# DeltaNet with soft-MoE slots on one core: two heads on tiles of 64x64 for three of TensorE's products, their weights made on GpSimd

## The chip, the cores and the metric

The kernel runs on one core of a Trainium2 chip. The metric is device time in microseconds (us) from the first to the last instruction, taken as the median of several executions. The engines are named as the profile names them: PE is TensorE's matmul, PEld its weight load, DVE is VectorE, ACT is ScalarE, POOL is GpSimd, SP is SyncE, which issues most transfers.

## The reference

Two blocks are computed one after the other, all in float32: attention with a delta rule, then a soft mixture of experts by slots.

```python
# attention: B=4, H=8, S=768, D=48
k_n = k / (np.linalg.norm(k, axis=-1, keepdims=True) + 1e-06)
for t in range(S):
    y[:, :, t] = q_t @ state
    v_old = k_t @ state
    state = state + beta_t * outer(k_t, v_t - v_old)
# bridge: x = y as (B*S, H*D) = (3072, 384)
# moe: 8 experts, 4 slots each, F = 1024
logits = x @ phi
d = softmax of logits over the 3072 rows          # for each of 32 slots
slot_input = d.T @ x                              # 32 x 384
slot_out[e] = relu(slot_input[e] @ w1[e]) @ w2[e]
c = softmax of logits over the 32 slots
out = c @ slot_out
```

(The loop's body is abridged; all heads and batches are computed alike.)

## The kernel before

Time is cut into 24 chunks of 32 steps; 4 chunks are a group, so there are 6 groups. Each 128-row tile holds 4 heads of 32 steps each, and a second index `u` of 8 counts 4 batches and 2 sets of heads. Within a chunk the delta rule is a triangular system. Its inverse (transposed, in `TT`) is made for all 32 systems of a group at once by elimination steps on VectorE, while the group before is in the recurrence.

The recurrence of one chunk, on TensorE, with ScalarE and VectorE reading its results:

```python
def rest():      # v minus what the state already gives for k
    state(0, ks)                                   # 16 matmuls, L413
    nc.vector.tensor_tensor(R, Vt.pop(cc), ks..., op=ALU.subtract)      # L420

def solve():     # L426: one matmul of 128x128 for each u, block-diagonal over 4 heads
    for u in range(U):
        nc.tensor.matmul(pw[:, u], lhsT=Tb[cc % NT][:, u, :], rhs=st["R"][:, u], ...)
    nc.scalar.activation(st["U"], pw, ACT.Copy)    # L429

def read():
    state(1, qs)                                   # L413, for q

def update():    # L439: the state's sum, 16 matmuls on 32 rows; then ACT reads it, L446
    ... lhsT=K[hs[h], b * G:(b + 1) * G, :]  (128 columns) ...

def outputs():   # L455: one matmul of 32x32 for each u and head
    ... lhsT=at[hs[h], b, g, 1, :], rhs=st["U"][hs[h], b * G + g] ...
```

`Tb` is a tile of zeros into whose four diagonal blocks POOL copies the inverse, chunk by chunk:

```python
def weights(cc):                                   # L394
    for h in range(4):
        r = slice(C * h, C * h + C)
        nc.gpsimd.tensor_copy(Tb[cc % NT][r, :, r], TT[n][r, c * U:(c + 1) * U, :])
```

The weights of the outputs, products of k and q, are masked in place on VectorE (`mask`, L246). An elimination step is a product (L321) and a subtraction (L324) on VectorE; the norms of k (L272 to L303), and two scalings of the matrix by `gamma` on POOL (L313), belong to it as well. The steps are spread over three places in each chunk by a table:

```python
share = [(0.0, 0.09, 0.12), (0.09, 0.09, 0.10), (0.09, 0.09, 0.10), (0.10, 0.07, 0.06)]
```

Each engine works through its instructions in order, so R of a chunk waits on VectorE until the steps put ahead of it are done.

One group later the routing follows: logits, the softmax over rows with a running maximum, and the sum of each slot's input. `heads` spreads the weights `pd` over four heads in `dr`, which holds zeros in the other heads' columns; `slots` then sums over rows:

```python
def heads():                                       # L567, 4 ACT instructions
    for h in range(4):
        nc.scalar.activation(dr[:, :, h, :], pd, ACT.Identity, scale=hm[:, h:h + 1])

def slots():                                       # L574, 16 matmuls of 128x128
    for c in range(GC):
        for b in range(B):
            nc.tensor.matmul(pa, lhsT=st["dr"][:, c * B + b]..., rhs=Yn[:, c, b, 0:GD + 1], ...)
```

After the last chunk the experts' weights w1 and w2 (1.5 MB for each expert and layer) are loaded into tiles that lie where attention's tiles lay; the two layers and the outputs follow (L847, L871, L897).

## Time and profile before

| what | before |
|---|---|
| median of 3 runs | 432.43 us (430.94 to 437.08) |
| span of the profiled execution | 435.1 us, mean granted TensorE clock 0.822 |
| first to last solution (L426) | 49.5 to 345.3 us |
| end of the last slots' sum (L574) | about 367 us |
| end of the last load of w2 | 407.7 us |

The profile is a page of one execution, and the trace behind it can be asked for single stretches. A row of the page's groups names line, engine, operation, what is written and read with its shape, and how often; then the busy time in all and the mean duration of one in ns; then how long the engine stood idle just before these instructions and what ended the waits. A row of a timeline gives start and duration in us, engine, line and operation, and in brackets the idle time before it and its releaser; `x16` means that 16 records were merged. A float32 matmul leaves two records, one for each pass through the array: the 16 records of a solution are 8 matmuls. The clock row (PEclk) shows for each of 40 equal slices of the span the clock that TensorE was granted, in tenths of full speed, with 9 for 90% or more.

### The profile page before, as it was taken

The page shows a single profiled execution, that of the slowest core. Times are in us where ns is not written, and L with a number is a line of the kernel's source. Part 1 is how long each engine was busy: PE and PEld are TensorE (multiplying, and loading weights), DVE is VectorE, ACT ScalarE, POOL GpSimd, SP SyncE. Part 2 cuts the span into 40 slices and gives each one's busy share as a digit, 9 for nine tenths or more (in the row PEclk, how much of TensorE's full clock was granted, in tenths as well). Part 3 has the DMA queues.
Part 4 walks back from the last instruction along what each step waited for, and adds up shares of the span by engine and source line. Part 5 has one row for each costly group of instructions (what it writes and reads, how often), then busy time and mean ns, then how long its engine had stood idle before and what let it go on. Part 6 is the DMA issues. An engine that isn't in the chain of part 4 may idle for free.

```text
span 435.1 us, 17057 instructions
## 1 busy us (share of the span) xinstructions
PE 344.3 (79%) x7583; PEld 281.7 (65%) x7583; DVE 226.4 (52%) x574; ACT 153.5 (35%) x308; POOL 103.4 (24%) x192
## 2 busy tenths in 40 slices
PE   4766888988686899779988799586997967876685
PEld 3545778877675897668977689475886856322143
DVE  8493684844858638775586756859502011101033
ACT  3342233455422645236452363331633621201022
POOL 9200702331504045040450404504151000000000
PEclk9999865698957879667995679856899986999595
DMA  6555455144413324342211101111400396799238
GB/s 102 92 89 87 80 86 84 26 67 73 83 23 50 57 43 93 77 106 41 36 22 20 22 10 17 17 20 20 148 3 3 110 431 241 278 427 427 119 127 307
DMA packets 85032, 45.29 MB, mean 104 GB/s; under 512 B 79424, under 2 KB 82656, under 8 KB 83040
## 3 DMA queue, kind: packets, MB, share of 16 engines
q1 hardware_dynamic: 83296, 43.86, 37.7%
q8 instruction: 59, 0.97, 0.9%
q0 software_dynamic: 576, 0.15, 0.3%
q10 hardware_dynamic: 1088, 0.20, 0.2%
q14 instruction: 13, 0.11, 0.1%
HBM read 39.47 MB, written 4.72 MB: 102 GB/s over the span
## 4 chain that ended last, share of the span: by engine, by line
PE 56%; DVE 13%; DMA 10%; ACT 8%; SPq 7%; issue 5%; POOL 1%; DVEq 0%; POOLq 0%; ACTq 0%
PE psR L426 13%; PE psS L439 8%; SPq L82 6%; PE pt L574 6%; DMA w2t<-in_moe_w_dram 5%; PE pt L208 5%; PE psY L455 4%; DVE pr L321 4%; DVE tt L324 3%; PE pso L871 3%; PE psR L413 3%; PE pt L473 3%; PE pt L237 2%; ACT dr L567 2%; DVE R L420 2%
## 5 line engine op out<-in xcount | busy, mean ns | idle before, releaser
L426 PE MATMUL psR<-R,Tb 128*128 128x48 f32 x384 | 61.5, 325 | 31.8 <-DVE R L420 31.8
L426 PEld LDWEIGHTS psR<-R,Tb 128*128 128x128 f32 x384 | 58.5, 241 | 34.8 <-issue 33.1
L321 DVE TENSOR_TENSOR pr<-tt,lb 128x31 f32<-128x31 f32 (+15 forms) x155 | 63.3, 409 | 9.5 <-POOL lb L313 5.2
L324 DVE TENSOR_TENSOR tt<-tt,pr 128x31 f32<-128x31 f32 (+15 forms) x155 | 63.9, 412 | 5.3
L394 POOL COPY Tb<-TT 32x256 f32<-32x256 f32 x96 | 40.8, 425 | 50.3 <-DMA V<-in_v_dram 22.9
L446 ACT ACTIVATE S<-psS 48x768 f32<-48x768 f32 x46 | 37.0, 804 | 30.3 <-PE psS L439 30.0
L429 ACT ACTIVATE U<-psR 128x384 f32<-128x384 f32 x24 | 11.8, 490 | 89.1 <-PE psR L426 78.4
L439 PE MATMUL psS<-U,K 32*128 32x96 f32 x736 | 36.8, 356 | 1.3 <-ACT U L429 0.8
L237 PE MATMUL pt<-KQ 48*32 48x64 f32 (+1 forms) x1792 | 28.0, 237 | 11.8 <-ACT KQ L224 4.7
L439 PEld LDWEIGHTS psS<-U,K 32*128 32x128 f32 x736 | 32.2, 256 | 6.8 <-ACT U L429 3.4
L237 PEld LDWEIGHTS pt<-KQ 48*32 48x32 f32 x1792 | 22.0, 118 | 19.3 <-ACT KQ L224 6.0
L420 DVE TENSOR_TENSOR R<-V,psR 128x384 f32<-128x384 f32 x24 | 13.2, 551 | 37.2 <-PE psR L413 27.4
L241 ACT ACTIVATE GQ<-pt 128x256 f32<-128x256 f32 (+1 forms) x56 | 16.7, 351 | 37.1 <-PE pt L237 37.1
L313 POOL TENSOR_TENSOR tt<-tt,gm 128x512 f32<-128x512 f32 x10 | 11.2, 1123 | 70.8 <-DVE tt L324 70.8
L455 PE MATMUL psY<-U,GQ 32*32 32x48 f32 x1536 | 27.4, 234 | 0.1
L574 PE MATMUL pt<-Y,dr 128*128 128x97 f32 x192 | 25.2, 295 | 2.5 <-ACT dr L567 2.5
L574 PEld LDWEIGHTS pt<-Y,dr 128*128 128x128 f32 x192 | 24.5, 210 | 3.0 <-ACT dr L567 2.8
L413 PE MATMUL psR<-S,KQ 128*32 128x96 f32 x768 | 25.1, 282 | 1.2 <-ACT S L446 1.2
L525 POOL TENSOR_TENSOR Call<-el,sm 128x128 f32<-128x128 f32 x6 | 2.4, 398 | 99.5 <-DVE sm L524 99.5
L455 PEld LDWEIGHTS psY<-U,GQ 32*32 32x32 f32 x1536 | 23.7, 129 | 3.4 <-issue 1.9
L413 PE MATMUL psY<-S,KQ 128*32 128x96 f32 x768 | 23.1, 264 | 0.7 <-issue 0.7
L386 POOL TENSOR_TENSOR V<-V,nT 128x384 f32<-128x384 f32 x24 | 21.0, 876 | 10.0 <-DMA Q<-in_q_dram 7.6
(142 smaller groups left out, 523.2 us busy)
## 6 DMA issues: line engine op xcount, KB each, us to landing
w2t<-in_moe_w_dram SPq DMA_DIRECT2D x8, 1536.0 KB, 17.2
w1t<-in_moe_w_dram SPq DMA_DIRECT2D x7, 1536.0 KB, 9.7
Q<-in_q_dram SPq DMA_DIRECT2D x96, 48.0 KB, 2.7
V<-in_v_dram SPq DMA_DIRECT2D x96, 48.0 KB, 2.4
out_dram<-ob SPq DMA_DIRECT2D x24, 192.0 KB, 2.4
K<-in_k_dram SPq DMA_DIRECT2D x92, 48.0 KB, 2.7
w1t<-in_moe_w_dram SPq DMA_DIRECT2D x3, 512.0 KB, 4.0
bb<-in_beta_dram POOLq DMA_DIRECT2D x16, 6.0 KB, 2.6
```

The costliest lines, as they stand in the source:

```text
L82: eng.dma_start(out=dst[C * h:C * h + C, :, 0:D], in_=src.rearrange("b (g h) s d -> h s (b g) d", h=4)[h, cc * C:(cc + 1) * C])
L237: nc.tensor.matmul(pg[g][rh, b], lhsT=kq[r, b, 0, rh], rhs=kq[r, b, a0:a1, rh], start=True, stop=True, skip_group_check=True)
L321: nc.vector.tensor_tensor(prv, tt[:, j, 0:m].unsqueeze(1).broadcast_to([P, w, m]), lb[:, j, j + 1:C].unsqueeze(2).broadcast_to([P, w, m]), ...
L324: nc.vector.tensor_tensor(tt[:, j + 1:C, 0:m], tt[:, j + 1:C, 0:m], prv, op=ALU.subtract)
L394: nc.gpsimd.tensor_copy(Tb[cc % NT][r, :, r], TT[n][r, c * U:(c + 1) * U, :])
L413: nc.tensor.matmul(dst[hs[h], b].rearrange("p g d -> p (g d)"), lhsT=kq[:, b, a, hs[h]], rhs=old[:, h, b, :], start=(b == 0), stop=False, ...
L420: nc.vector.tensor_tensor(R, Vt.pop(cc), ks.rearrange("p b g d -> p (b g) d"), op=ALU.subtract)
L426: nc.tensor.matmul(pw[:, u], lhsT=Tb[cc % NT][:, u, :], rhs=st["R"][:, u], start=(u == 0), stop=True, skip_group_check=True)
L439: nc.tensor.matmul(psS[:, h, b * GD:(b + 1) * GD], lhsT=K[hs[h], b * G:(b + 1) * G, :].rearrange("p g d -> p (g d)"), rhs=st["U"][hs[h], b ...
L446: nc.scalar.activation(new[r, :, :, g * D:(g + 1) * D], psS[r, :, 0:B * GD].rearrange("p h (b g e) -> p h b g e", b=B, g=G)[:, :, :, g], A ...
L455: nc.tensor.matmul(qs[hs[h], b, g], lhsT=at[hs[h], b, g, 1, :], rhs=st["U"][hs[h], b * G + g], start=False, stop=True, skip_group_check=True)
L574: nc.tensor.matmul(pa, lhsT=st["dr"][:, c * B + b].rearrange("p h s -> p (h s)"), rhs=Yn[:, c, b, 0:GD + 1], start=(c == 0 and b == 0), st ...
```

## The change

It uses the fact that the block-diagonal weights of four heads are half empty even where only two heads are looked at together. Rows 0 to 63 (two heads) and rows 64 to 127 (the other two) become two products of 64x64 that lie on different rows and columns of the array, in place of one of 128x128 (solution, slots) or of four of 32x32 (outputs).

- The solution's and the outputs' weights are made by POOL, in one product each for a chunk: the inverse times `own`, which says which of a row's two columns blocks is its own head's; and the k-q products times `tri`, which holds the causal mask in the own block. The mask on VectorE and the cleared tiles of 128 columns go away.
- The slots' weights need two instead of four instructions on ScalarE. The sum is split into two parts, placed in the last chunk of a group and in the first chunk of the next.
- The update loads 112 instead of 128 columns (the last 16 held padding).
- The next group's norms: the transposition of its products (`spread`) is placed inside the last chunk of a group, the root at that chunk's end, and the rest ahead of R of the next chunk. Before, all of it stood after the chunk and behind that R.
- The table of shares is set anew, and a few preparations in the first four chunks change places.

The diff, cut to its core (cuts are marked with `[...]`):

```diff
+    own = cpool.tile([P, 2], F32, name="own")
+    nc.vector.tensor_reduce(own, hm.rearrange("p (y x) -> p x y", x=2), axis=AX.X, op=ALU.add)
+    tri = cpool.tile([P, 2, C], F32, name="tri")
 [...]
-    Tb = [wk.tile([P, U, P], F32, name=f"Tb{i}", bufs=1) for i in range(NT)]
-    for t in Tb:
-        nc.vector.memset(t, 0.0)
+    Tb = [wk.tile([P, U, 2, C], F32, name=f"Tb{i}", bufs=1) for i in range(NT)]
+    Ab = [wk.tile([P, U, 2, C], F32, name=f"Ab{i}", bufs=1) for i in range(NT)]
 [...]
-        def mask(self):
-            a = GQ[self.n][:, self.c, :, :, 1, :].rearrange("p b g t -> p (b g) t")
-            nc.vector.tensor_tensor(a, a, tri.unsqueeze(1).broadcast_to([P, U, C]), op=ALU.mult)
 [...]
     def weights(cc):
-        for h in range(4):
-            r = slice(C * h, C * h + C)
-            nc.gpsimd.tensor_copy(Tb[cc % NT][r, :, r], TT[n][r, c * U:(c + 1) * U, :])
+        nc.gpsimd.tensor_tensor(
+            Ab[cc % NT], wide(GQ[n][:, c, :, :, 1, :].rearrange("p b g t -> p (b g) t")),
+            tri.unsqueeze(1).broadcast_to([P, U, 2, C]), op=ALU.mult)
+        nc.gpsimd.tensor_tensor(
+            Tb[cc % NT], wide(TT[n][:, c * U:(c + 1) * U, :]),
+            own.unsqueeze(1).unsqueeze(3).broadcast_to([P, U, 2, C]), op=ALU.mult)
 [...]
         def solve():
             for u in range(U):
-                nc.tensor.matmul(pw[:, u], lhsT=Tb[cc % NT][:, u, :], rhs=st["R"][:, u],
-                                 start=(u == 0), stop=True, skip_group_check=True)
+                for y in range(2):
+                    nc.tensor.matmul(pw[half[y], u], lhsT=T[y][:, u], rhs=st["R"][half[y], u],
+                                     start=(u == 0), stop=True, skip_group_check=True)
 [...]
-                        lhsT=K[hs[h], b * G:(b + 1) * G, :].rearrange("p g d -> p (g d)"),
+                        lhsT=K[hs[h], b * G:(b + 1) * G].rearrange("p g d -> p (g d)")[:, 0:DP + D],
 [...]
         def outputs():
-                    for h in range(4):
-                        nc.tensor.matmul(qs[hs[h], b, g], lhsT=at[hs[h], b, g, 1, :],
-                                         rhs=st["U"][hs[h], b * G + g],
+                    for y in range(2):
+                        nc.tensor.matmul(qs[half[y], b, g], lhsT=at[y][:, u],
+                                         rhs=st["U"][half[y], u],
 [...]
         def heads():
-            for h in range(4):
-                nc.scalar.activation(dr[:, :, h, :], ..., ACT.Identity, scale=hm[:, h:h + 1])
+            for x in range(2):
+                nc.scalar.activation(dr[:, :, x, :], ..., ACT.Identity, scale=own[:, x:x + 1])
-        def slots():
+        def slots(cs):
+                    for y in range(2):
+                        r = slice(64 * y, 64 * y + 64)
+                        nc.tensor.matmul(pa[r], lhsT=st["dr"][r, c * B + b]..., rhs=Yn[r, c, b, 0:GD + 1], ...)
 [...]
-                dict(end=[slots]),
-                dict(head=[collect])]
+                dict(end=[lambda: slots((0, 1))]),
+                dict(head=[lambda: collect(True)], mid=[lambda: slots((2, 3))],
+                     vec=[lambda: collect(False)])]
 [...]
-    share = [(0.0, 0.09, 0.12), (0.09, 0.09, 0.10), (0.09, 0.09, 0.10), (0.10, 0.07, 0.06)]
+    share = [(0.0, 0.14, 0.15), (0.10, 0.10, 0.10), (0.09, 0.09, 0.08), (0.10, 0.05, 0.0)]
 [...]
-        at[0][1] += [f["norms"]]
+        at[0][0] += [f["norms"]]
 [...]
         drain(EL[c][1])
+        if follow and x > GC:
+            follow[0]["spread"]()
         solve()
 [...]
-        for _ in range(min(2, len(masks))):
-            masks.pop(0).mask()
```

## The prediction

> **What bounds the kernel now.** I read the table of engines and the granted clock first, then the costliest groups, then single chunks in the timeline, then the waits of the DMA queue.
>
> ```profile
> PE 344.3 (79%) x7583; PEld 281.7 (65%) x7583; DVE 226.4 (52%) x574; ACT 153.5 (35%) x308; POOL 103.4 (24%) x192
> PEclk9999865698957879667995679856899986999595
> L426 PE MATMUL psR<-R,Tb 128*128 128x48 f32 x384 | 61.5, 325 | 31.8 <-DVE R L420 31.8
> L394 POOL COPY Tb<-TT 32x256 f32<-32x256 f32 x96 | 40.8, 425 | 50.3 <-DMA V<-in_v_dram 22.9
> L313 POOL TENSOR_TENSOR tt<-tt,gm 128x512 f32<-128x512 f32 x10 | 11.2, 1123 | 70.8 <-DVE tt L324 70.8
> L574 PE MATMUL pt<-Y,dr 128*128 128x97 f32 x192 | 25.2, 295 | 2.5 <-ACT dr L567 2.5
> ```
>
> TensorE is the busiest engine, and the solution (L426) its costliest line: 61.5 us. But before it TensorE also idles 31.8 us for R, which VectorE makes (L420). So two things bound the recurrence in turns: TensorE's own work, and VectorE's queue, in which R stands behind elimination steps of the next group. The clock row dips to 0.5 to 0.6 where TensorE waits. Two chunks of group 3 show both cases (columns: start, duration, engine, line):
>
> ```profile
> 208.76 0.19 DVE L321 TENSOR_TENSOR pr<-tt,lb 128x31 f32<-128x31 f32 x1
> ...
> 211.75 3.71 PE L574 MATMUL pt<-Y,dr 128*128 128x97 f32 x32
> ...
> 217.64 1.99 PE L426 MATMUL psR<-R,Tb 128*128 128x48 f32 x16
> ...
> 218.78 2.05 POOL L313 TENSOR_TENSOR lb<-lb,gm 128x512 f32<-128x512 f32 x2 [3.36 <-DVE gm L296]
> ...
> 219.87 1.02 DVE L321 TENSOR_TENSOR pr<-tt,lb 128x31 f32<-128x31 f32 x1 [1.04 <-POOL lb L313]
> ...
> 220.43 1.15 PE L439 MATMUL psS<-U,K 32*128 32x96 f32 x32
> ...
> 221.51 0.88 PE L455 MATMUL psY<-U,GQ 32*32 32x48 f32 x64
> ...
> 230.08 3.62 PE L426 MATMUL psR<-R,Tb 128*128 128x48 f32 x16 [3.60 <-DVE R L420]
> ```
>
> A solution takes 1.99 us at full clock and 3.62 after a wait that lowered it. The last lines that matter are of the DMA queue, at the end of attention:
>
> ```profile
> 344.47 22.66 SPq L192 DMA_DIRECT2D w2t<-in_moe_w_dram  x4
> 367.17 12.17 SPq L186 DMA_DIRECT2D w1t<-in_moe_w_dram  x4
> ...
> SPq L192 <- PE pt L574: 19.8, 1, 19.8
> ```
>
> The fourth load of w2 waits 19.8 us for the last slots' sum (its tile lies where dr was), and the w1 behind it waits too. DMA falls idle near 365 us; the stage after ends about 68 us (435.1 - 367.2) after that sum.
>
> **What the skill says.** (1) "TensorE: Matmul & The Clock Gate", section "LDWEIGHTS (loading the stationary operand)": the load's time goes with its columns, not its rows. The trace agrees: each f32 matmul is recorded as two passes, and 16 passes of 128 columns in 1.99 us are 124 ns each, for 48 moving columns only. (2) "TensorEngine Tiling (Array Packing)", section "Key Properties": tiles load and multiply independently, and a change of tile mode drains the array. The trace agrees with the first: the update's 32 passes also load 128 columns, but on four row tiles, and take 1.15/32 = 36 ns each, an overlap of 124/36 = 3.4 out of 4, or 86%. I see no gap of a drain in it. (3) "GPSIMD Engine Reference", section "Specifications": POOL shares its SBUF interface with VectorE where that has two SBUF inputs. The trace agrees: the product of 31 elements takes 0.19 us alone and 1.02 us beside POOL's two-input L313; it ends when that does. Beside the one-input copies a step of 60 elements takes 0.40 instead of 0.22.
>
> **The change part by part.** Warm means full clock, cold half.
>
> *Solution.* 8 matmuls of 128x128 become 16 of 64x64 on two tiles: 32 passes with 64 columns, 62 ns alone; at 86% overlap of two, 62/1.72 = 36 ns, so 32 x 36 = 1.15 us. Saves 0.84 warm. Cold, 3.62/16 = 226 ns gives 113/1.72 = 66, or 2.1 us, and saves 1.5. Before, 16 of the 24 are warm or nearly so.
>
> *Outputs.* 32 matmuls of 32x32 (64 passes, 0.88 us, 14 ns each) become 16 of 64x64: by the same sum 1.15, a loss of 0.27 warm, about 0.5 cold. It follows the update, so it runs beside ScalarE's eviction of the state (2 x 0.80 us, L446), for which the next chunk waits anyway; I count half.
>
> *Update.* 112 instead of 128 columns: 12% of 1.15, a gain of 0.14 (0.25 cold).
>
> *Slots' sums.* 32 passes of 3.71 us become 64 passes of 64 columns. The 97 moving columns now count: the median matmul of L847 (512 columns) takes 592 ns, of L871 (384) 486, so 0.83 ns a column, 80 ns for 97; two tiles at 86% give 47 ns, x64 = 3.0 us, a gain of 0.7 in each of 6 groups (about 1.0 in the last, cold one: 6.38 before). The sum is also cut in two, so that at most 1.5 us stands ahead of the next state.
>
> *heads.* dr needs 2 instead of 4 ACT instructions of 0.61 us: 1.2 us less in each group. Five of these stretches lie on the chain of waits.
>
> *Mask.* 24 DVE products of 0.44 us (10.5 us) go away.
>
> *Weights on POOL.* 4 copies of 0.425 us (1.70 a chunk) become two products of 128x512. L313 has that size and a broadcast operand: 1.05 to 1.12 us. So 2.2 us a chunk, 24 x 0.5 = 12 us more on an engine that is 24% busy: no bound. The cost is VectorE's: stopped for 2.2 us a chunk, where the copies cost it about 0.7 (four steps stretched by 0.18). Less the mask, that is 2.2 - 0.7 - 0.44 = 1.0 us more VectorE time a chunk, in the 20 chunks with elimination. I take half of it as falling into gaps of VectorE.
>
> *Norms and shares.* Transposing the next group's products and its norms goes into the last slot of a group and ahead of R. That frees some 3.5 us between R of chunk 0 and the first step (216.4 to 219.9 above), but 39% instead of 30% of the steps now stand before R of chunk 1: 9% of a group's elimination (127 us / 5 = 25 us) is 2.3 us. The rest is a gain of about 1 us, which the stops by POOL (five two-input products in a row there) take back.
>
> *Sum.* The time between solutions of successive chunks in group 3 was 12.4, 17.1, 13.9 and about 10 us. I estimate: first interval +0.5 (VectorE bound, nothing gained from TensorE), second -1.5 (cold solution, part kept by VectorE), third -2 (cold solution, heads), fourth -1 (solution, shorter slots, norms ahead of R): -4 for each of groups 1 to 3. Group 0: -3 (warm solutions, less outputs). Group 4, with few preparations beside it: -5, as 3.7 us of slots leave the last interval. Group 5 has no elimination, its solutions and heads count in full: 3 x 0.8 + 1.2 less the moved half sum, -3. Together -23. From the last solution to the last slots' sum: solution 0.85, slots 1.9 and 1.0, heads 1.2: -5. The loads move along with it; in the built program the first four w2 loads no longer wait for that sum, but the w1 loads behind them still wait for the first layer, so I count no more than the 5. 432.4 - 28 = **404 us**.
>
> **Rivals.** (a) *VectorE becomes the bound.* For it: TensorE waits for R already 13 times, and POOL's stops come on top. Then groups 1 to 4 gain nothing, and what stays is groups 0 and 5 and the end: about 420. If POOL's products run one after the other and always hit elimination, 20 x 1.0 us more would leave 425 or worse. Against it: in group 3 VectorE was busy 35.7 of 53 us. (b) *64x64 tiles don't overlap.* Then 32 x 62 ns are again 2 us, the outputs double, and the change loses: some 440. Against it: the update's 36 ns. (c) *Less TensorE work, lower clock.* Gaps in TensorE are where the clock falls; faster matmuls make more of them, and cold stages give back perhaps 5 to 8 us: about 411. (d) *The weights' loads are freed*, as the wait for the slots' sum goes: DMA then has no gap after the last solution, and the end gains up to 9 instead of 5: 400. If shorter PE waits also remove cold stretches, 390.
>
> **Range and chances.** (a) in part and (c) speak for less gain, (d) for more, so I put the range nearly even around the sum: 390 to 420. Only (b), or (a) with all its force, comes near no change: faster 0.91, within 2% 0.06, slower 0.03.
>
> **What would show it.** Solution: a median stage of 32 passes near 1.15 us, against 2 us by (b); its total near 34 us instead of 61.5. Outputs up from 27 to near 33 us. Slots near 19 us instead of 25. POOL near 115 us busy, in 48 products of about 1.08 us. Idle time for R before the solution at or above 31.8 us; much above says (a). A mean clock below 0.82 says (c). The stage from the last slots' sum to the end stays 68 us if (d) is wrong. The prediction fails most likely in the middle of groups 1 to 4, where I split VectorE's stops by guess.

## The result and the profile after

The changed kernel takes **402.74 us** (median of 4 runs, 399.97 to 406.66), the kernel before 434.75 us in the runs beside it (430.94 to 438.26). The ratio is **0.926**, with a 95% interval of 0.916 to 0.936. The span of the profiled execution fell from 435.1 to 398.2 us and the mean granted clock rose from 0.822 to 0.843. Disturbed runs are left out of all ratios, so a ratio is not always the quotient of the two medians, and as the profiled execution of before was one of its longer ones, differences between the two traces overstate the gain by some microseconds.

The rows of the page: engines, granted clock, and the groups of the elimination (its product and its subtraction), the solution, POOL's two products and the outputs.

```profile
PE 310.5 (78%) x7391; PEld 247.8 (62%) x7391; DVE 235.4 (59%) x554; ACT 147.8 (37%) x296; POOL 120.5 (30%) x144
PEclk9999975996865899758998689856799978999685
L320 DVE TENSOR_TENSOR pr<-tt,lb 128x31 f32<-128x31 f32 (+15 forms) x155 | 76.0, 490 | 7.2 <-POOL lb L312 2.9
L323 DVE TENSOR_TENSOR tt<-tt,pr 128x31 f32<-128x31 f32 (+15 forms) x155 | 70.0, 452 | 5.3
L434 PE MATMUL psR<-R,Tb 64*64 64x48 f32 x768 | 31.4, 238 | 31.7 <-DVE R L427 31.7
L396 POOL TENSOR_TENSOR Tb<-TT,own 128x512 f32<-128x512 f32 x24 | 26.4, 1102 | 30.0 <-ACT TT L376 25.3
L393 POOL TENSOR_TENSOR Ab<-GQ,tri 128x512 f32<-128x512 f32 x24 | 32.1, 1336 | 4.0 <-ACT GQ L244 4.0
L464 PE MATMUL psY<-U,Ab 64*64 64x48 f32 x768 | 32.5, 243 | 0.0
```

The elimination in the page of before:

```profile
L321 DVE TENSOR_TENSOR pr<-tt,lb 128x31 f32<-128x31 f32 (+15 forms) x155 | 63.3, 409 | 9.5 <-POOL lb L313 5.2
L324 DVE TENSOR_TENSOR tt<-tt,pr 128x31 f32<-128x31 f32 (+15 forms) x155 | 63.9, 412 | 5.3
```

The slots' sum stands in the table of groups that keeps shapes apart:

```profile
L585 PE MATMUL pt<-Y,dr 64*64 64x97 f32 x384 | 20.8, 266 | 1.8 <-ACT dr L576 1.4 <-ACT yT L483 0.5
```

Three things are to be seen. The solution's total fell from 61.5 to 31.4 us. TensorE waits for R as long as before (31.7 us, before 31.8). VectorE's eliminations grew although their number and sizes did not: both rows together (L320 and L323) are 146.0 us busy, before 127.2. VectorE has no mask any more (10.5 us), and yet its total rose from 226.4 to 235.4.

Where the time went is read from the starts of the solutions in the timeline. Each group has four intervals from one solution to the next; the mean over groups 1 to 3, in us:

| interval | before | after | difference |
|---|---|---|---|
| first | 12.5 | 14.2 | +1.6 |
| second | 16.7 | 14.8 | -1.9 |
| third | 13.5 | 9.4 | -4.0 |
| fourth | 11.7 | 8.9 | -2.8 |
| start of the first to start of the last solution, all 24 chunks | 294.1 | 264.1 | -30.0 |
| start of the last solution to the end | 91.5 | 85.2 | -6.3 |

The first interval is the only one that grew. The timeline of group 3 (start, duration, engine, line; rows of other engines left out) shows what fills it:

```profile
199.75 1.02 DVE L320 TENSOR_TENSOR pr<-tt,lb 128x31 f32<-128x31 f32 x1 [0.59 <-POOL lb L312]
200.68 0.83 POOL L385 TENSOR_TENSOR V<-V,nT 128x384 f32<-128x384 f32 x1
200.81 0.77 DVE L323 TENSOR_TENSOR tt<-tt,pr 128x31 f32<-128x31 f32 x1
201.47 1.27 POOL L393 TENSOR_TENSOR Ab<-GQ,tri 128x512 f32<-128x512 f32 x1
201.62 1.20 DVE L320 TENSOR_TENSOR pr<-tt,lb 128x60 f32<-128x60 f32 x1
202.70 1.04 POOL L396 TENSOR_TENSOR Tb<-TT,own 128x512 f32<-128x512 f32 x1
202.85 0.96 DVE L323 TENSOR_TENSOR tt<-tt,pr 128x60 f32<-128x60 f32 x1
...
204.66 0.25 DVE L323 TENSOR_TENSOR tt<-tt,pr 128x87 f32<-128x87 f32 x1
```

POOL's products with two inputs follow one another, and VectorE gets exactly one instruction done beside each: it starts about 0.15 us after POOL's and ends with it. Instructions that take 0.2 us alone take 0.77 to 1.20 us. It is so in the whole trace: 64 of POOL's two-input instructions ran beside the elimination, in each exactly one step began, and that one ended 0.04 to 0.28 us after it. The hold does not meet every VectorE instruction:

```profile
226.46 1.21 POOL L396 TENSOR_TENSOR Tb<-TT,own 128x512 f32<-128x512 f32 x1
226.70 0.54 DVE L427 TENSOR_TENSOR R<-V,psR 128x384 f32<-128x384 f32 x1
...
227.16 0.77 DVE L320 TENSOR_TENSOR pr<-tt,lb 128x231 f32<-128x231 f32 x1
```

R, which reads one operand from PSUM, ends long before POOL's product, in the 0.52 to 0.56 us that it always takes; the step behind it, with both operands in SBUF, again ends after it (0.77 us, alone 0.40). POOL's memset that follows at 227.61 for 0.98 us, which reads nothing, holds no step: the two that began in it took 0.40 and 0.39 us.

The timeline also shows what became of the third chunk's solution in group 3 (the number in the bracket is the wait for R ahead of it); first in the kernel before, then in the changed one, with a solution of group 4 that follows a long wait:

```profile
247.20 3.62 PE L426 MATMUL psR<-R,Tb 128*128 128x48 f32 x16 [2.96 <-DVE R L420]
```

```profile
227.38 1.14 PE L434 MATMUL psR<-R,Tb 64*64 64x48 f32 x32 [1.70 <-DVE R L427]
...
258.95 1.95 PE L434 MATMUL psR<-R,Tb 64*64 64x48 f32 x32 [6.61 <-DVE R L427]
```

The wait is shorter and the clock stayed up (granted 1.00 in the stage of 1.14 us, 0.50 in those of 3.62 and 1.95): 2.48 us less for a stage that at full clock loses 0.85. It is so in groups 1 to 3 alike, where this solution went from 3.62 to 1.14, 1.24 and 1.14 us. Which solution stays warm is not fixed, though. A kernel that differs from the changed one only in the loads (below) had it the other way round in groups 2 and 3: second solutions of 1.14 and 1.13 us, third ones of 1.94 and 1.95. The second and third interval together are 29.7 to 30.9 us before, 23.3 to 24.7 after and 23.8 to 24.5 in that kernel: the sum is what the change shortened, and its split between the two belongs to one execution.

At the end of attention the loads of the weights are of interest, from the timeline of the DMA queue and from its waits (us in total, times, longest):

```profile
314.21 1.94 SPq L195 DMA_DIRECT2D w2t<-in_moe_w_dram  x4
```

```profile
SPq L189 <- PE ph L855: 25.5, 1, 25.5
```

All four first loads of w2 are now issued 1.2 us after the last solution; none waits for the last slots' sum. The w1 behind them wait 25.5 us for the first layer, as the prediction said they would. Of the 6.3 us that the end gained, 5.1 lie between the last solution and the end of the last slots' sum (18.0 us, before 23.1) and 1.2 behind it (67.2, before 68.4).

### The profile page after: what moved, and what is told of

Read it like the earlier page. It is cut to its first block, busy times and chain, and to the rows that moved or that the text cites. A ratio compares the mean times of both kernels' runs of the same rounds, so it can differ in the third digit from the quotient of the medians.

```text
span 398.2 us, 16603 instructions
## 1 busy us (share of the span) xinstructions
PE 310.5 (78%) x7391; PEld 247.8 (62%) x7391; DVE 235.4 (59%) x554; ACT 147.8 (37%) x296; POOL 120.5 (30%) x144
## 4 chain that ended last, share of the span: by engine, by line
PE 34%; DVE 26%; SPq 12%; issue 11%; DMA 9%; ACT 3%; POOL 3%; DVEq 0%; POOLq 0%; ACTq 0%
SPq L82 11%; DVE pr L320 10%; DVE tt L323 8%; DMA w2t<-in_moe_w_dram 5%; PE psR L434 5%; PE psS L447 3%; PE pso L879 3%; PE pt L482 3%; PE pt L585 3%; PE pt L211 3%; PE psY L464 3%; DVE R L427 2%; PE psR L420 2%; PE ph L855 2%; PE pt L567 2%
## 5 line engine op out<-in xcount | busy, mean ns | idle before, releaser
L320 DVE TENSOR_TENSOR pr<-tt,lb 128x31 f32<-128x31 f32 (+15 forms) x155 | 76.0, 490 | 7.2 <-POOL lb L312 2.9
L323 DVE TENSOR_TENSOR tt<-tt,pr 128x31 f32<-128x31 f32 (+15 forms) x155 | 70.0, 452 | 5.3
L434 PE MATMUL psR<-R,Tb 64*64 64x48 f32 x768 | 31.4, 238 | 31.7 <-DVE R L427 31.7
L434 PEld LDWEIGHTS psR<-R,Tb 64*64 64x64 f32 x768 | 28.7, 153 | 35.1 <-issue 24.1
L396 POOL TENSOR_TENSOR Tb<-TT,own 128x512 f32<-128x512 f32 x24 | 26.4, 1102 | 30.0 <-ACT TT L376 25.3
L393 POOL TENSOR_TENSOR Ab<-GQ,tri 128x512 f32<-128x512 f32 x24 | 32.1, 1336 | 4.0 <-ACT GQ L244 4.0
L464 PE MATMUL psY<-U,Ab 64*64 64x48 f32 x768 | 32.5, 243 | 0.0
L447 PE MATMUL psS<-U,K 32*112 32x96 f32 x736 | 31.1, 321 | 0.7 <-ACT U L437 0.6
L464 PEld LDWEIGHTS psY<-U,Ab 64*64 64x64 f32 x768 | 29.2, 157 | 3.0 <-issue 1.2
L447 PEld LDWEIGHTS psS<-U,K 32*112 32x112 f32 x736 | 26.8, 223 | 5.5 <-ACT U L437 1.9
L211 PE MATMUL pt<-ident,Q 128*128 128x128 f32 x76 | 23.1, 341 | 1.3 <-DMA Q<-in_q_dram 0.9
L420 PEld LDWEIGHTS psR<-S,KQ 128*32 128x32 f32 x768 | 20.3, 129 | 3.8 <-issue 2.1
## 6 DMA issues: line engine op xcount, KB each, us to landing
w1t<-in_moe_w_dram SPq DMA_DIRECT2D x7, 1536.0 KB, 10.6
```

The source lines that it names most:

```text
L211: nc.tensor.transpose(dst, self.src[a][:, b * G:(b + 1) * G, :].rearrange("p g d -> p (g d)"), ident)
L320: nc.vector.tensor_tensor(prv, tt[:, j, 0:m].unsqueeze(1).broadcast_to([P, w, m]), lb[:, j, j + 1:C].unsqueeze(2).broadcast_to([P, w, m]), ...
L323: nc.vector.tensor_tensor(tt[:, j + 1:C, 0:m], tt[:, j + 1:C, 0:m], prv, op=ALU.subtract)
L393: nc.gpsimd.tensor_tensor(Ab[cc % NT], wide(GQ[n][:, c, :, :, 1, :].rearrange("p b g t -> p (b g) t")), tri.unsqueeze(1).broadcast_to([P, ...
L396: nc.gpsimd.tensor_tensor(Tb[cc % NT], wide(TT[n][:, c * U:(c + 1) * U, :]), own.unsqueeze(1).unsqueeze(3).broadcast_to([P, U, 2, C]), op= ...
L420: nc.tensor.matmul(dst[hs[h], b].rearrange("p g d -> p (g d)"), lhsT=kq[:, b, a, hs[h]], rhs=old[:, h, b, :], start=(b == 0), stop=False, ...
```

## The experiments

**What is to be told apart.** Theory A is the prediction's own account: TensorE's shorter pieces bring the gain, the solution's most of all, and slots, `heads` and the placing of the norms bring the rest. Theory H says that POOL's products with two inputs, which make the new weights, hold VectorE and cost back a part. Among the rivals: VectorE's queue bounds so much that the shorter solution is worth little and the new order brings the gain; the gain lies in the loads at the end; and H's cost is nothing because VectorE has gaps. All times are medians of runs beside the kernel before on the same chip; ratios are to that kernel, with 95% intervals. "After" is the changed kernel (402.74 us, 0.926).

### The solution alone

The kernel before, with only the solution on tiles of 64x64; POOL still makes its weights by four copies.

```diff
-    Tb = [wk.tile([P, U, P], ...)]
+    Tb = [wk.tile([P, U, 2, C], ...)]
-            nc.gpsimd.tensor_copy(Tb[cc % NT][r, :, r], TT[n][r, ...])
+            nc.gpsimd.tensor_copy(Tb[cc % NT][r, :, h % 2, :], TT[n][r, ...])
-                nc.tensor.matmul(pw[:, u], lhsT=Tb[cc % NT][:, u, :], rhs=st["R"][:, u], ...)
+                for y in range(2):      # rows r = 64y to 64y + 63
+                    nc.tensor.matmul(pw[r, u], lhsT=Tb[cc % NT][r]...[:, u], rhs=st["R"][r, u], ...)
```

> The kernel before with the solution alone on 64x64 tiles; its weights are still four copies on POOL, now into tiles of 64 columns, everything else as before. Theory A (the solution's time on TensorE is most of the gain, but is lost where VectorE's queue makes R late): a solution takes 1.14 us warm and 1.94 cold; 16 warm ones save 0.85 each and 8 cold ones 1.7, 27 us in all, of which the interval from chunk 0 to chunk 1 of groups 1 to 4 keeps nothing: some 18 us less than before, ratio 0.96. Rival B (VectorE holds nearly all of it, and the change's gain comes from mask, norms and shares): under 8 us less, ratio above 0.98.

Measured: 415.0 us beside 435.61, ratio 0.956 (0.946 to 0.966). The group of the solution, and the queue's longest wait for TensorE:

```profile
L428 PE MATMUL psR<-R,Tb 64*64 64x48 f32 x768 | 32.7, 244 | 35.3 <-DVE R L420 35.2
```

```profile
SPq L192 <- PE pt L579: 20.9, 1, 20.9
```

The solution lost 28.8 us of busy time, and the time from the first to the last solution fell from 294.1 to 264.5 us in the traces: nearly all of it arrived. That is as much as the whole change brought there (264.1). In group 3 the intervals went from 12.4, 17.1, 13.8, 9.9 to 12.5, 14.2, 10.6, 9.5: nothing in the first, which VectorE sets, about 3 in each of the two middle ones (on the mean of groups 1 to 3, 1.6 in the second, 2.8 in the third and 1.7 in the fourth). But the time from the last solution to the end grew from 91.5 to 96.9 us. The tiles of `Tb` are half as large, the tiles behind them moved, and now it is the first load of w2 that waits for the last slots' sum, where before it was the fourth. From the end of that sum to the end of the kernel it is 75.2 us, before 68.4. So theory A holds, with a loss of 5 us at the end that has nothing to do with the recurrence.

### The old norms and shares

After, with the table of shares, the place of the norms and of `spread` as before.

```diff
-    share = [(0.0, 0.14, 0.15), (0.10, 0.10, 0.10), (0.09, 0.09, 0.08), (0.10, 0.05, 0.0)]
+    share = [(0.0, 0.09, 0.12), (0.09, 0.09, 0.10), (0.09, 0.09, 0.10), (0.10, 0.07, 0.06)]
-        at[0][0] += [f["norms"]]
+        at[0][1] += [f["norms"]]
-        at[3][1] += f["steps"][i:] + [lambda: f["scale"](1)]
-        at[3][2] += [lambda: f["back"](1)]
+        at[3][2] += f["steps"][i:] + [lambda: f["scale"](1), lambda: f["back"](1)]
-        if follow and x > GC:
-            follow[0]["spread"]()          # and again at the chunk's end, as before
```

> The changed kernel with the next group's transposition, root and norms and the table of shares put back as before; all tiles, weights and slots as changed. Theory A (the re-ordering is worth little, as the elimination steps are only moved from one interval to another): at most 8 us slower than the changed kernel, ratio to before about 0.94; the interval from chunk 0 to chunk 1 of a group stays near 14 us. Rival B (the re-ordering carries the gain in the second half of each group): 15 us slower or more, ratio 0.96 or above.

Measured: 404.3 us, ratio 0.928 (0.919 to 0.937). By the medians the new order is worth 1.6 us, which these intervals don't tell from nothing. A rival by which the order brings the gain is out.

### The old slots and heads

After, with the slots' sum in one piece of 128x128 and `heads` in four ScalarE instructions.

```diff
-            for x in range(2):
-                nc.scalar.activation(dr[:, :, x, :], ..., scale=own[:, x:x + 1])
+            for h in range(4):
+                nc.scalar.activation(dr[:, :, h, :], ..., scale=hm[:, h:h + 1])
-                    for y in range(2):
-                        nc.tensor.matmul(pa[r], lhsT=st["dr"][r, c * B + b]..., rhs=Yn[r, c, b, 0:GD + 1], ...)
+                    nc.tensor.matmul(pa, lhsT=st["dr"][:, c * B + b]..., rhs=Yn[:, c, b, 0:GD + 1], ...)
-                dict(end=[lambda: slots((0, 1))]),
-                dict(head=[lambda: collect(True)], mid=[lambda: slots((2, 3))], vec=[lambda: collect(False)])]
+                dict(end=[slots]),
+                dict(head=[collect])]
```

> The changed kernel with the slots' sums and their weights put back: 16 matmuls of 128x128 in one piece, dr made by four ACT instructions. Theory A (heads and slots are on the path in part): from the last solution to the last slots' sum 5 us more, and about 1 us in each group before: 8 us slower, ratio about 0.945. Rival B (the slots' sum hides beside VectorE's queue everywhere but at the end): 4 us slower, ratio about 0.935.

Measured: 417.22 us, ratio 0.960 (0.951 to 0.969): 14 us, more than expected. The waits of the queue changed again:

```profile
SPq L195 <- PE pt L583: 19.1, 1, 19.1
```

The fourth load of w2 waits for the slots' sum again, but that costs little. The time from the last solution to the end is 90.0 us instead of 85.2; 4.0 of these 4.8 us lie ahead of the end of the last slots' sum (22.0 instead of 18.0), where the longer sums and the two more instructions of `heads` stand and where 5 were expected, and only 0.8 behind it. The other 12.0 us of the two traces' difference lie in the recurrence (276.1 instead of 264.1): the fourth intervals, where the whole sum stands ahead of the next state, grew by about 2, the third by about 1, where two more instructions of `heads` stand. This kernel differs from the one with the solution alone by the rest of the change without the slots: POOL's products, the tiles of outputs and update, the mask, the order. And its recurrence is 11.6 us longer than there (264.5). So something in that rest costs as much as the slots bring. The next runs look for that.

### Outputs on 32x32 again

```diff
-                    for y in range(2):
-                        nc.tensor.matmul(qs[half[y], b, g], lhsT=at[y][:, u], rhs=st["U"][half[y], u], ...)
+                    for h in range(4):
+                        nc.tensor.matmul(qs[hs[h], b, g], lhsT=Ab[cc % NT][hs[h], u, h % 2, :], rhs=st["U"][hs[h], u], ...)
```

> The changed kernel with the outputs put back on 32x32 tiles (64 passes instead of 32), read from the own blocks of the same POOL product. Theory A (outputs run beside ScalarE's eviction of the state, so their 0.26 us a chunk are off the path): the same time within 2 us as the changed kernel, ratio 0.92 to 0.93, and the outputs' busy time falls from 32.5 to about 27 us. Rival B (outputs lie on the path): 5 us faster than the changed kernel, ratio about 0.915.

Measured: 405.29 us, ratio 0.932 (0.924 to 0.939).

```profile
L464 PE MATMUL psY<-U,Ab 32*32 32x48 f32 x1536 | 23.7, 214 | 0.0
```

8.8 us less of TensorE (23.7 instead of 32.5) bring no gain: the outputs run beside ScalarE's eviction of the state and lie off the path. They are not where these 12 us went.

### POOL's product for the solution, written twice

```diff
+        nc.gpsimd.tensor_tensor(Tb[cc % NT], wide(TT[n]...), own..., op=ALU.mult)   # a second time, same result
```

> The changed kernel with the product for the solution's weights written twice on POOL in each chunk: one more two-input product of 1.05 us a chunk, with nothing gained from it. Theory H (VectorE, which bounds the first two intervals of a group, is held for as long as POOL has a two-input product, and gets one instruction in between): the first interval goes from 14.2 to 15.2 us, the second from 15.3 to 16.5 or more, 9 us more in all over five groups, ratio about 0.945; the eliminations' busy time (146 us) rises by some 15. Rival (POOL has room, its products are off the path): no change, ratio 0.926.

Measured: 411.74 us beside 435.58, ratio 0.944 (0.937 to 0.952), 9 us more by the medians and 8 by the ratios, as H expected. The subtraction of the elimination in the table of groups:

```profile
L323 DVE TENSOR_TENSOR tt<-tt,pr 128x31 f32<-128x31 f32 (+15 forms) x155 | 80.7, 520 | 5.3
```

VectorE does the same work, and its eliminations are busy 157.8 us instead of 146.0 (77.1 and 80.7). On the mean of groups 1 to 3 the first interval went from 14.2 to 15.0 us, as expected, the second only from 14.8 to 15.4. From the first to the last solution it is 4.6 us in the traces (268.7 instead of 264.1); another 2.1 lie behind the last solution, where nothing was changed, and the traces of other kernels with the same loads differ there as much. So about 5 of these 8 or 9 us lie, in the traces, where H puts them; the rest is not placed. An engine that is 30% busy costs time when it does more: not by being late itself, but by holding VectorE.

### Tb by copies with one input

After, with POOL making the solution's weights by four copies, as in the first experiment.

```diff
-        nc.gpsimd.tensor_tensor(Tb[cc % NT], wide(TT[n]...), own..., op=ALU.mult)
+        for h in range(4):
+            nc.gpsimd.tensor_copy(Tb[cc % NT][r, :, h % 2, :], TT[n][r, c * U:(c + 1) * U, :])
```

> The changed kernel with the solution's weights made by four copies with one input each on GpSimd, into tiles of 64 columns that are cleared once, in place of one product with two inputs. Theory H (a two-input instruction on GpSimd holds VectorE's two-input instructions for its whole length, a copy only stretches them): some 0.3 us less for each of 24 chunks where VectorE bounds them, eliminations' busy time below 146 us, about 2 us less in total, ratio about 0.92 beside 0.926 of the change. Rival (copies hold VectorE as long as a product does): no change in the eliminations' busy time, ratio 0.926 or above.

Measured: 397.85 us, ratio 0.919 (0.914 to 0.924). From the timeline of group 3:

```profile
199.59 1.27 POOL L395 TENSOR_TENSOR Ab<-GQ,tri 128x512 f32<-128x512 f32 x1
199.74 1.20 DVE L322 TENSOR_TENSOR pr<-tt,lb 128x60 f32<-128x60 f32 x1
200.80 1.73 POOL L400 COPY Tb<-TT 32x256 f32<-32x256 f32 x4
200.97 0.30 DVE L325 TENSOR_TENSOR tt<-tt,pr 128x60 f32<-128x60 f32 x1
201.31 0.44 DVE L322 TENSOR_TENSOR pr<-tt,lb 128x87 f32<-128x87 f32 x1
201.78 0.42 DVE L325 TENSOR_TENSOR tt<-tt,pr 128x87 f32<-128x87 f32 x1
```

Beside the product, one VectorE instruction in 1.2 us; beside the copies, one after another of 0.30 to 0.44 us. That looks as if copies only stretched VectorE's steps, as theory H has it. The single records, which the row `x4` merges, say otherwise: the four copies ended at 201.19, 201.64, 202.09 and 202.53, and the steps that had begun in them at 201.27, 201.74, 202.19 and 202.66, each 0.08 to 0.13 us after its copy. In the whole trace of the kernel before, 56 copies ran beside the elimination; in 50 of them exactly one step began, in none two, and no step that began in a copy ended before it did (in this kernel's own trace one step began in 41 of 51, none in 9, and two in one, a copy of 0.65 us). A step of 60 elements ended 0.07 us after a copy there, 0.08 us after a product in the changed kernel. So the number of inputs is not what counts: a copy holds VectorE just as a product does, for as long as it lasts. It lasts only 0.39 us, so that four steps pass in 1.73 us, where the product of 1.0 to 1.1 us lets one pass.

This also gives the size. The four steps above took 1.58 us, alone 0.99 (0.22, 0.25, 0.25 and 0.27), a loss of 0.59 us for a chunk; the one beside the product took 0.96 instead of 0.22, a loss of 0.74. The difference of 0.15 us in each of 20 chunks is, as an estimate, 3.0 us. The eliminations' busy time falls to 143.3 us, 2.7 less, and the gain from the first to the last solution is 1.4 us. The copies take 0.7 us longer than the product. The interval of the ratio overlaps that of the change. Theory H was right that copies cost less, and wrong in why.

### The weights taken off POOL, one and then both

First the solution's weights by two ScalarE instructions, then the outputs' weights on VectorE as well.

```diff
-        nc.gpsimd.tensor_tensor(Tb[cc % NT], wide(TT[n]...), own..., op=ALU.mult)
+        for x in range(2):
+            nc.scalar.activation(Tb[cc % NT][:, :, x, :], TT[n]..., ACT.Identity, scale=own[:, x:x + 1])
 # second kernel, besides:
-        nc.gpsimd.tensor_tensor(Ab[cc % NT], wide(GQ[n]...), tri..., op=ALU.mult)
+        nc.vector.tensor_tensor(Ab[cc % NT], wide(GQ[n]...), tri..., op=ALU.mult)
```

> The changed kernel with the solution's weights made by ScalarE: two instructions of 128x256 a chunk, scaled by own, in place of POOL's product. Theory H (hold of VectorE): first interval 14.2 to 13.1 us, second 15.3 to 14 us, 9 us less in all, ratio about 0.905; the eliminations' busy time falls from 146 to about 130. Rival (what counts is ScalarE, through which the solution, state and outputs pass): 24 x 0.76 us more on it cancel the gain or turn it into a loss of up to 5 us, ratio 0.925 to 0.94.

> As the run with the solution's weights on ScalarE, and the outputs' weights made by VectorE itself instead of POOL (one product of 128x512 a chunk, estimated at 0.65 us from the 0.69 that one of this size took at group 0). Theory H: doing it costs VectorE 0.65 us where POOL's product of 1.34 us held it for 1.2 or more, so some 2 us a group less than with the ScalarE weights alone, ratio about 0.895. Rival (the hold only falls into gaps of VectorE at that place): VectorE's own time is added, 3 us a group more, ratio 0.915 or more.

Measured: 399.76 us, ratio 0.917 (0.911 to 0.922), and 392.07 us, ratio 0.899 (0.893 to 0.906). From the groups of the first kernel and of the second:

```profile
L397 ACT ACTIVATE Tb<-TT,own 128x256 f32<-128x256 f32 x48 | 21.6, 503 | 0.1
```

```profile
L320 DVE TENSOR_TENSOR pr<-tt,lb 128x31 f32<-128x31 f32 (+15 forms) x155 | 64.7, 417 | 7.1 <-POOL lb L312 2.9
L393 DVE TENSOR_TENSOR Ab<-GQ,tri 128x512 f32<-128x512 f32 x24 | 16.7, 697 | 0.0
```

The first brought 3 to 4 us where 9 were expected, and its interval overlaps that of the change. The eliminations fell from 146.0 to 137.8 us busy, where 130 were expected. On the mean of groups 1 to 3 the first interval went from 14.2 to 13.4, while the second stayed (14.7, after 14.8). In the traces' recurrence the product doubled and the product removed come out alike, 4.6 us more and 4.1 less (260.0 us). What the two instructions cost on ScalarE in turn is not told apart. The second kernel gives VectorE 16.7 us of work more and is 8 us faster still by the medians, 3.9 in the recurrence of the traces (256.1 us), as the eliminations fall to 123.6 us. On POOL the same product took 1336 ns, on VectorE 697. In the timeline the step that took 0.96 us beside POOL's product is then back at what it needs:

```profile
198.16 0.22 DVE L323 TENSOR_TENSOR tt<-tt,pr 128x60 f32<-128x60 f32 x1
```

Together 11 us by the medians, 8.0 in the recurrence. That is of the size of the 11.6 us which the rest of the change, without the slots, had cost; the two are no exact counterparts, as here the hold by the old copies is gone as well, while VectorE makes the outputs' weights.

### The loads of the weights

After, with `dr` and Y in a pool of their own behind the others, and two more of the first w1 loads ahead.

```diff
+    wl = att.enter_context(tc.tile_pool(name="wl", bufs=1))     # opened last; dr and Y move there
-            load_w1(e, wp2, 4)
+            load_w1(e, wp2, 6)
```

> The changed kernel with six instead of four buffers for w1 and with dr and Y in a pool that lies behind the others, so that nine loads go out after the last outputs, and only the last w1 waits for the first layer. Theory A (after the last solution the loads' own rate is the next bound, 14 loads of 3.66 us with no gap ending 2 to 3 us earlier than the 58.7 us after the last solution that they take now): 2 to 3 us less, ratio about 0.92. Rival (the end follows the computing chain alone): no change.

Measured: 400.78 us, ratio 0.921 (0.916 to 0.926): no gain beyond the intervals. The gap of DMA after the last solution is gone, but the loads start later (317.5 instead of 314.2 us, after the last outputs), and the last w2 arrives at 371.9 instead of 371.7 us. The time from the last solution to the end is 84.8, before 85.2. In all fourteen traces of this case the kernel ends 26.5 to 27.5 us after the last w2 has landed: the loads bound the end. Here they land without a gap, one in 3.7 us, but begin later. What an earlier start is worth, the next kernels show.

### The best version

Both kernels of weights off POOL, with the loads' pool, `U` and `Ab` in it too, the norms of one group behind R; then with fewer steps in the first interval; then with fewer still.

```diff
-        at[0][0] += [f["norms"]]
+        at[0][n == 2] += [f["norms"]]
 # second kernel
-    share = [(0.0, 0.14, 0.15), (0.10, 0.10, 0.10), (0.09, 0.09, 0.08), (0.10, 0.05, 0.0)]
+    share = [(0.0, 0.12, 0.13), (0.10, 0.10, 0.10), (0.09, 0.09, 0.09), (0.10, 0.08, 0.0)]
 # third kernel
+    share = [(0.0, 0.11, 0.12), (0.10, 0.09, 0.09), (0.10, 0.10, 0.10), (0.10, 0.09, 0.0)]
```

> All that the runs point to, together: the solution's weights on ScalarE, the outputs' weights on VectorE, the norms of the third group after R of the fifth chunk (there R waits for them), six buffers for w1, and dr, Y, U and the outputs' weights in a pool that lies behind the others, so that loads no longer wait for the last outputs. From the run with both weights moved (ratio 0.899): 2 us less at the fifth chunk, 3 us less at the end, ratio about 0.888. Rival (the end follows the computing chain, and the fifth chunk waits for its products anyway): ratio 0.899 as there.

> As the combined run, with the table of shares moved by 4% of the elimination from the first interval of a group to its last two (0.25, 0.30, 0.28, 0.17 by slots). Theory (the first interval is bounded by VectorE, at 13.1 us, and the last two have room): first interval 1 us shorter in each of five groups, the last 0.5 longer, 2 to 3 us less in all, ratio about 0.882. Rival (the last interval is bounded by VectorE too, with transposition and norms in it): no change or 2 us more.

> The combined kernel with its new shares (378.67 us), with more of the elimination's steps taken out of the first interval and put into the third and fourth. Theory (the first interval, still 12.15 us in group 3, is held by VectorE's steps while the others have room): first interval about 11.3 us, second about 0.5 us shorter, third and fourth about 0.5 us longer, some 2 us less in all, ratio to the kernel before about 0.875. Rival (the third and fourth intervals, 9.38 and 8.74 us, are already held by VectorE too): what the first gains, the third and fourth lose, and the time stays within 1 us or grows; ratio 0.88 or above.

Measured: 385.52 us, ratio 0.898 (0.890 to 0.907); 378.67 us, ratio 0.880 (0.871 to 0.889); 377.99 us, ratio 0.871 (0.865 to 0.876). From the waits of TensorE in the second of them:

```profile
PE psR L435 <- DVE R L428: 24.6, 11, 4.8
```

The wait for R, 31.7 us in 16 pieces after the change, is 24.6 us in 11. In group 3 the first interval went from 14.17 to 12.16 us. Taking out still more steps shortened it to 11.27 as expected, but the second grew from 11.91 to 12.95 (the trace of this last kernel is of its longest execution, 382.92 us): the two medians lie 0.7 us apart, which can't be told from nothing. Moving more steps brought nothing that can be told. The version beats both kernels, by some 24 us the changed one. The first of the three is 6.5 us below the kernel with both weights off POOL (392.07) by the medians, at the same ratio: the kernel before ran between 426.05 and 440.56 us beside it, so the ratio decides little here. The traces tell its two edits apart. From the last solution to the end it takes 80.3 us instead of 85.3, where 3 us were expected: with `U` and `Ab` moved too, one load more goes out ahead of the last solution, the others do not wait for the last outputs, and the last w2 lands 52.9 us after the last solution instead of 58.8. From the first to the last solution it takes 257.0 us instead of 256.1, so the later norms, of which 2 us were expected, brought nothing. The new shares bring some 7 us by the medians; no run with them took as long as any without.

## Why the prediction was right, and where it was right by luck

The predicted 404 us was met within 1.3 us, in part by luck: beside it the kernel before took 434.75 us and not 432.4, so that the gain was 32.0 us, where 28 were forecast. Of the intervals in groups 1 to 3, the first lost more than said (1.6 us instead of 0.5), the second gained what was said (1.9, expected 1.5), and the third and fourth gained more (4.0 and 2.8, expected 2 and 1). Two steps were mis-sized, with errors of opposite sign: what the shorter solution brings in the third and fourth interval, and what POOL's products cost in the first.

- *Solution.* A stage of 32 passes took 1.14 us warm and 1.94 cold, by the sum 1.15 and 2.1. Its total is 31.4 us, expected 34. The trace of this case fits the Trainium skill's page "TensorEngine Tiling (Array Packing)", section "Key Properties", by which different tiles can load weights and multiply in parallel: the 86% taken from the update hold for two tiles on the diagonal too. Rival (b) is out.
- *What of it counts.* This is the first step that failed. The prediction took -2 for the third interval, slots and `heads` included, and -1 for the fourth. The solution alone brought 2.8 and 1.7 there, and its 28.8 us of busy time arrived nearly whole. The third interval gained most (4.0), as its solution became warm: 2.5 us less in each of groups 1 to 3. The estimate for a cold solution (3.62 to 2.1) was for one that stays cold; it did not count that the wait ahead of it could shrink, here from 2.96 to 3.90 us in these groups to 1.63 to 1.82. That the shorter wait is what keeps the clock up is likely, not shown; and as the kernel with only the loads changed had the second solutions warm and the third cold, 2.5 us belong to the pair of intervals and not to the third alone.
- *Clock.* By rival (c) gaps would grow and the clock fall. The mean clock rose: 0.80 to 0.85 in the four runs of the changed kernel, 0.80 to 0.835 in the seven of before beside the first experiments. That a stage is cold after a long gap was seen; that faster matmuls make more such gaps was not, as the idle time for R stayed the same.
- *Weights on POOL.* This is the second step. POOL's total was near the estimate (120.5, expected 115), though the outputs' product takes 1336 ns and not the 1080 taken for both. It was named that VectorE's time is what counts, at 1.0 us more for each of 20 chunks with half in gaps, which is 10 us. VectorE's busy time grew by 9.0 us in all, not by 20 (the eliminations by 18.8, from 127.2 to 146.0, less the mask), and what it cost was about as said: 8.0 us of the recurrence came back with both products off POOL, and 11.6 us is what the rest of the change cost without the slots. Wrong was where: the first interval grew by 1.6, expected 0.5. The Trainium skill's page "GPSIMD Engine Reference", section "Specifications", names the contention for VectorE's instructions with two SBUF inputs, and the trace agrees, as R with its operand in PSUM is not held; the size came only from the runs.
- *Outputs.* A stage takes 1.14 us, expected 1.15; the total 32.5, expected 33. Half of it was counted as a loss; the run with the old outputs shows none within its interval.
- *Update.* 1.04 us instead of 1.15, expected 1.01.
- *Slots' sums and heads.* Two stages of 1.55 us, expected 1.5; in total 20.8, expected 19; the last, cold sum 5.44, expected about 5.4. What was expected of undoing them was about 8; it costs 14. The part after the last solution was sized well (4.0 of 5 expected, and 0.8 for the load that waits again); the recurrence pays 12.0 where about 1 us a group was expected.
- *Norms and shares.* Expected about nothing, measured 1.6 us by the medians, not clear of nothing.
- *Groups.* Group 0 gained 4.2 (expected 3), groups 1 to 3 7.1 on the mean (9.0, 4.6 and 7.8; expected 4 each), group 4 3.2 (expected 5), group 5 1.3 (expected 3). In group 4 VectorE bounds the first interval too, which grew from 12.7 to 14.2 us; in group 5 the first interval, which now holds half of the slots' sum, gained nothing (7.7 and 8.0).
- *The end.* Expected -5, measured -6.3, of which 5.1 lie where they were expected, ahead of the end of the last slots' sum. Behind it the time is 67.2 us (before 68.4), so rival (d) is wrong for this change: the loads of w1 still wait for the first layer. Its idea holds where the loads are really freed: the first of the best versions, whose loads neither wait for the last outputs nor start late, takes 62.2 us there, 5.1 less than the kernel with both weights off POOL.
- *Rival (a)*, VectorE as the bound, is right for the first interval of each group with elimination and partly for the second. TensorE waited for R 31.8 us before and 31.7 after, ahead of the second solutions 16.0 and 18.8, ahead of the third 14.1 and 8.9, and ahead of the first of groups 2 to 4 0.2 and 2.6. The prediction saw the risk, and its guess of half of the stops in gaps was too mild for the first interval.

What stays open: how much of the change's recurrence each part has, to the microsecond. Solution -25 to -30, slots and `heads` -12 and at the end -5, the weights on POOL +8 to +12 are read from single undoings, each traced in one execution, and parts that meet at the same wait don't add up exactly. Open is also what decides whether a solution behind a wait runs cold.

## What to carry to other kernels

An engine's busy share says nothing of what it does to another engine: before moving work to an idle POOL, look in the timeline at what VectorE's instructions take beside POOL's, and count each POOL instruction that reads SBUF as VectorE time for its whole length, less the one step that passes beside it. Short ones then cost less than one long one. When one engine waits in one stretch and another in the next, price a shorter stage interval by interval, and look at several executions before giving a gain of clock to one stage. After any change of a tile's size, look at the waits of the DMA queue again, as tiles behind it have moved and other loads wait. Where the loads bound the end, an earlier start counts as much as a missing gap.

## What the runs showed of the hardware

- Beside a POOL instruction that reads SBUF, with one input or two, an elimination step of VectorE with both operands in SBUF ended only after it: 0.04 to 0.28 us after in all 64 products of the changed kernel, 0.07 to 0.28 us after in the 50 copies of before in which a step began (0.2 us alone became 0.77 to 1.20 us beside a product, 0.30 to 0.44 beside copies of 0.39, in the kernel with four of them). R, with one operand in PSUM, was not held (0.54 to 0.56 us inside five products), and a memset on POOL held no step.
- Two 64x64 float32 tiles on the diagonal took 1.14 us for 32 passes, 36 ns each, where a 128x128 pass with the same 48 moving columns took 124 ns.
- In groups 1 to 3 of before and after, a solution ran at or near full clock where TensorE had waited at most 2.46 us for R (but for one of 3.20 us without any wait), and wholly or partly at the lower one from 2.96 us on. Other traces of this case break such a rule: 1.13 us, full clock, after a wait of 3.16 in the kernel with the loads moved; 1.95 after 2.47 beside 1.14 after 2.48 in one trace of the best version. The wait's length alone does not decide.
- The same product of 128x512 took 1336 ns on POOL and 697 ns on VectorE.
- The kernel ended 26.5 to 27.5 us after the last load of w2 had landed, in all fourteen traces. Halving a tile's size, in the kernel with the solution alone, cost 5 us at the end by changing which load waited 20.9 us for which instruction.
